# Five moves in the written order of a kernel that joins decaying linear attention to a two-layer feed-forward part: an opening half unit, state decays, key decays and two sums

## The chip, the cores and the metric

The kernel runs on one core of a Trainium2 chip. The metric is device time in microseconds (us); a time of the kernel is the median of several runs. The five engines of the core are named as the profile names them: PE (TensorE, with PEld for its loads of stationary operands), DVE (VectorE), ACT (ScalarE), POOL (GpSimd) and SP (SyncE, which only issues transfers here). Each works through its own queue of instructions in order, and they meet at semaphores.

## The reference

There are two parts, the second fed by the first. The first is attention with a decay in place of a softmax, over q, k, v of shape (4, 8, 768, 64), in blocks of rows with a state that is handed on from block to block:

```
intra = (q_block @ k_block.T * Dmask) @ v_block          # Dmask[i, j] = lam ** (i - j) where i >= j, else 0
inter = (q_block * lam ** (pos + 1)) @ kv_state
out   = intra + inter
kv_state = lam ** block * kv_state + (k_block * lam ** (block - 1 - pos)).T @ v_block
```

The result, laid out as x of shape (3072, 512), goes through a feed-forward part with w_in (512, 2048), w_out (2048, 512) and one slope alpha for each of the 2048 columns:

```
h = x @ w_in
g = maximum(h, 0) + alpha * minimum(h, 0)
out = g @ w_out                                          # float32
```

## The kernel before, in words

**Tiling.** The 3072 rows are cut into 6 chunks of 512 (256 positions of two batches). Attention is cut into 24 units, n = 4c + 2 bi + hh: chunk c, one of its two batches, one half of the heads. Units 4c to 4c+3 together make the input x (`xT`) of chunk c. A unit has two blocks of 128 positions. The feed-forward columns are cut into 16 groups f of 128.

**A unit of attention** is made of these steps, each a small function:

- `load`, `cast` (L307, to 16 bits), `transposes` or `transposed` (q and k turned), `decayed` (L420, the queries with their decay, tile `qdT`) and `key_decayed` (L363, the keys with theirs, tile `kdec`); the last two run mostly on GpSimd.
- `cluster(old, new)`: TensorE's products, in this order: `inter(old)` (L440, queries by state R into the bank `acc`), `score_products(new)` (L458 or L470, into the bank `s`), `intra(old)` (L504, masked scores by values into `acc`) and `state_products(new)` (L524, decayed keys by values into `acc`). There is one bank for `s` and one pair for `acc`.
- `masked` (L485): VectorE multiplies the scores by the decay mask, tile `sm`.
- `attended` (L303): ScalarE copies the result out of `acc` into `xT`.
- `kept` (L553): VectorE adds the new state to the decayed old one, tile R, in up to four instructions; for the first chunks ScalarE copies the first of them (L563). In the opening `state1(n, bank, a)` does the state of one block alone in another bank, started with zeros (L584), so that it needn't wait for `acc`.

**The feed-forward part.** `up(c, f)` makes the products of one column group (L631, four 128x512 products; with a batch given, a half unit of four 128x256 ones), `relu` takes the negative part on ScalarE (L644, tile m) and `act` forms g on VectorE (L655, from m and the product's bank). The products with w_out of the first two chunks are plain (`down`, L668). From chunk 2 on they are done in Strassen's way with seven products of half size in place of eight: `product(c, i, b)` (L825), fed by sums of parts of g (`g_sum`, L808) and of w_out (`weight_sum`, L791). `g_sum(c, i, j, eng)` makes sum i of the column groups 2j and 2j+1 and their partners 2j+8 and 2j+9: i = 1 is called S1 here, i = 2 is S2, which is S1 less another part of g (`g<-s,g` in the profile) and so comes behind S1, i = 3 and 4 are differences of two parts (`g<-g`). The engine is a parameter: "G" for GpSimd, "V" for VectorE. The results go out by `evacuated` (L881, L884) and `written` (L863). In the last chunk the products with w_in are done in the same way (L736).

**The order.** No scheduler orders the work. Some 950 lines of calls, one below the other, are the program (`tc.manual_schedule()`); what a call issues goes to the end of the queue of its engine. To move a call therefore moves its instructions within their own engine's queue, and another engine feels it only through waits. The lines around the five places:

```
    cluster(14, 15)
    attended(14, "A")
    masked(15)
    kept(15)
...
    g_sum(2, 3, 3, "G")
    relu(3, 2, None)
    act(3, 9, None)
    g_sum(2, 2, 3, "G")
    weight_sum(3, 0)
    decayed(18)
```

On-chip accumulators: the banks are named `op`, `tk` and `h` (two buffers) for the feed-forward part and `acc` and `s` for attention; the second product into a bank waits until its last reader is done.

Of the kernel before, what the change touches and what calls it, by code (L numbers as in the profile page):

```python
# [11 lines left out]
def kernel(  # L12
# [72 lines left out]
    def load(c, bi, x, half=None, queue="S"):  # L85

        pb, b = c // 2, 2 * (c % 2) + bi
        if (c, bi) not in raws:
            raws[c, bi] = {}
        if x not in raws[c, bi]:  # L90
            raws[c, bi][x] = (rawv_pool if x == "v" else raw_pool).tile(
                [128, H, 2 * D], fp32, tag=f"{x}raw", name=f"{x}raw"
            )
        heads = ds(0, H) if half is None else ds(4 * half, 4)
        i = "kqv".index(x)
        if x == "k" and c >= HC:
            for a in range(2):
                for f in range(2):
                    nc.sync.dma_start(
                        out=raws[c, bi][x][ds(64 * a, 64), heads, ds(D * f, D)],  # L100
                        in_=k[b, heads, ds(pb * W + L * a + 64 * f, 64), :].rearrange("h p d -> p h d"),
                    )
            return
        (nc.gpsimd if queue == "G" else nc.sync).dma_start(
            out=raws[c, bi][x][:, heads, :],
            in_=(k, q, v)[i][b, heads, ds(pb * W, W), :].rearrange("h (p e) d -> p h (e d)", e=2),
        )
# [193 lines left out]
    def copy_on(eng, out, in_):  # L301
        if eng == "A":
            nc.scalar.activation(out, in_, AF.Copy)  # L303
        elif eng == "V":
            nc.vector.tensor_copy(out=out, in_=in_)
        else:
            nc.gpsimd.tensor_copy(out=out, in_=in_)  # L307
# [8 lines left out]
    def cast(n, name, eng):  # L316
        t = T.setdefault(n, {})
        if name == "v16":
            t[name] = v_of(n)
            c, bi, hh = units[n]  # L320
            copy_on(eng, t[name].rearrange("p h e d -> p h (e d)"), raws[c, bi]["v"][:, ds(4 * hh, 4), :])
            return
        if "qk16" not in t:
            t["qk16"] = half_pool.tile([128, 2, 2, 4, D], fp16, tag="qk16", name="qk16")
        copy_on(eng, t["qk16"][:, int(name == "k16")], raw_of(n)[name])

    V = {}

    def v_of(n):
        c, bi, hh = units[n]  # L330
        if (c, bi) not in V:
            V[c, bi] = v_pool.tile([128, H, 2, D], fp16, tag="v16", name="v16")
        return V[c, bi][:, ds(4 * hh, 4)]
# [24 lines left out]
    def key_decayed(n, eng="G"):  # L358
        hh = units[n][2]
        kr = raw_of(n)["k16"]  # L360
        decay = hdecay if units[n][0] >= HC else kdecay
        kdec = kv_pool.tile([128, 2, 4, D], fp16, tag="kdec", name="kdec")
        engine(eng).tensor_tensor(  # L363
            out=kdec,
            in0=kr,
            in1=decay[:, ds(4 * hh, 4), :].rearrange("p h e -> p e h").unsqueeze(3).to_broadcast([128, 2, 4, D]),
            op=ALU.mult,
        )
        T.setdefault(n, {})["kdec"] = kdec
# [108 lines left out]
    def masked(n):  # L478
        t = T[n]
        t["sm"] = sm_pool.tile([128, 2, 2, 2, L], fp16, tag="sm", name="sm")  # L480
        if units[n][0] >= HC:
            out, in0 = (y.rearrange("p a h x j -> p (a h) (x j)")[:, :, 0:192] for y in (t["sm"], t["s"]))
            nc.vector.tensor_tensor(out=out, in0=in0, in1=HM[units[n][2]], op=ALU.mult)
            return
        nc.vector.tensor_tensor(  # L485
            out=t["sm"].rearrange("p a h x j -> p (a h) x j"),
            in0=t["s"].rearrange("p a h x j -> p (a h) x j"),
            in1=mask_of(units[n][2]),
            op=ALU.mult,
        )  # L490
# [42 lines left out]
    def attended(n, eng):  # L533
        co, bo, ho = units[n]
        if co not in XT:
            XT[co] = xt_pool.tile([128, NHP, 2, 2, L], fp16, tag="xT", name="xT")
        copy_on(
            eng,
            XT[co][:, ds(2 * ho, 2), :, bo, :].rearrange("p h e (a j) -> p a (h e) j", a=2),
            acc[:, :, 0:256].rearrange("p a (he j) -> p a he j", j=64),  # L540
        )
# [24 lines left out]
    def cluster(old, new):  # L566

        if old is not None:
            inter(old)
        if new is not None:  # L570
            score_products(new)
        if old is not None:
            intra(old)
        if new is not None:
            state_products(new, kv_acc, old is None)

    def kept(n):
        states(n, kv_acc)
# [23 lines left out]
    def state1(n, bank, a):  # L602

        t = bank_of(bank, "kv")
        kv = {a: t[:, 0:256].rearrange("p (h l d) -> p h l d", h=2, l=2)}
        beside(kv[a], a)
        state_products(n, kv, False, (a,))
        states(n, kv, (a,))

    G = {}  # L610
# [15 lines left out]
    def up(c, f, bi=None, bank="h"):  # L626
        h_ps = spare[bank] if isinstance(bank, int) else bank_of(bank, "h_ps")
        n = CH if bi is None else W
        for gi in range(NHP):
            x = XT[c][:, gi]  # L630
            nc.tensor.matmul(  # L631
                h_ps[:, 0:n] if bi is None else h_ps[:, 0:n].rearrange("p (e j) -> p e j", e=2),
                lhsT=w_in_sb[:, gi, ts(f, 128)],
                rhs=x.rearrange("p e b j -> p (e b j)") if bi is None else x[:, :, bi, :],
                start=(gi == 0),
                stop=(gi == NHP - 1),
            )
        P[c, f, bi] = h_ps

    def relu(c, f, bi=None):  # L640
        h_ps = P[c, f, bi]
        n = CH if bi is None else W
        m = m_pool.tile([128, CH], fp32, tag="m", name="m")
        nc.scalar.activation(m[:, 0:n], h_ps[:, 0:n], AF.Relu, scale=-1.0)  # L644
        P[c, f, bi] = (m, h_ps)

    def act(c, f, bi=None):
        m, h_ps = P.pop((c, f, bi))
        g = g_of(c, f)
        if bi is None:  # L650
            g, mv, hv = g.rearrange("p e b j -> p (e b j)"), m, h_ps
        else:
            g = g[:, :, bi, :]
            mv, hv = (y[:, 0:W].rearrange("p (e j) -> p e j", e=2) for y in (m, h_ps))
        nc.vector.scalar_tensor_tensor(  # L655
            out=g, in0=mv, scalar=oma[:, f : f + 1], in1=hv, op0=ALU.mult, op1=ALU.add
        )
# [4 lines left out]
    def down(c, t, part, bank):  # L662
        if part == 0:
            O[c, t] = bank_of(bank, "o_ps")
        o_ps = O[c, t]
        n = NF // 4
        for f in range(part * n, part * n + n):
            nc.tensor.matmul(  # L668
                o_ps,
                lhsT=lhs(c, f, t),  # L670
                rhs=w_out_sb[:, f, :],
                start=(f == 0),
                stop=(f == NF - 1),
            )
# [122 lines left out]
    def g_sum(c, i, j, eng, b=None):  # L797

        a11, a12, a21, a22 = [part_of(c, j, half, e, b) for e in range(2) for half in range(2)]
        s1 = sums[3].rearrange("p f (b j) -> p f b j", b=2)[:, ds(2 * j, 2)]  # L800
        s1 = s1.rearrange("p i b j -> p i (b j)") if b is None else s1[:, :, b]
        out, in0, in1, op = {
            1: (s1, a21, a22, ALU.add),
            3: (a21, a11, a21, ALU.subtract),
            2: (a11, s1, a11, ALU.subtract),
            4: (a12, a12, a11, ALU.subtract),
        }[i]
        engine(eng).tensor_tensor(out=out, in0=in0, in1=in1, op=op)  # L808
# [169 lines left out]
    cluster(2, None)  # L978
    attended(2, "A")
    load(1, 1, "q", 1, "G")  # L980
    state1(2, "op", 1)
    state1(3, "tk", 1)
    state1(0, "h", 1)
    cast(4, "q16", "G")
    cluster(3, None)
    attended(3, "A")
    load(1, 1, "k", 1, "G")
    cast(5, "q16", "G")
    up(0, 4, 0, "h")
    relu(0, 4, 0)  # L990
    act(0, 4, 0)
    cast(4, "k16", "G")
    load_v16(5)
# [330 lines left out]
    cluster(13, 14)  # L1324
    attended(13, "A")
    g_sum(2, 3, 0, "G")
    g_sum(2, 3, 1, "G")
    kept(14)
    key_decayed(16, "G")
    down(1, 3, 3, "op")  # L1330
    copied(1, 3)
    masked(14)
# [10 lines left out]
    act(2, 5, None)  # L1343
    cluster(14, 15)
    attended(14, "A")
    masked(15)
    kept(15)
    relu(2, 6, None)
    transposes(16, "D", False)
    cast(19, "k16", "A")  # L1350
# [59 lines left out]
    relu(3, 9, None)  # L1410
    g_sum(2, 3, 3, "G")
    relu(3, 2, None)
    act(3, 9, None)
    g_sum(2, 2, 3, "G")
    weight_sum(3, 0)
    decayed(18)
    act(3, 2, None)
# [92 lines left out]
    act(3, 7, None)  # L1510
    product(2, 4, 0)
    product(2, 4, 1)
    g_sum(3, 3, 2, "V")
    evacuated(2, 4)
    written(2, 4)
    up(3, 15, None, "h")
# [1 line left out]
    relu(3, 15, None)  # L1518
    product(3, 1, 0)
    act(3, 15, None)  # L1520
    g_sum(3, 1, 3, "G")
    up(4, 0, None, "h")
    g_sum(3, 3, 3, "G")
# [351 lines left out]
```

## Time and profile before

| | |
|---|---|
| runs (us) | 205.24, 203.91, 203.53; median 203.91 |
| the profiled execution | 204.43 us, of which the span from the first to the last instruction is 202.6 us |
| granted TensorE clock | 0.999 |
| busy share of the span | PE 97%, PEld 65%, DVE 82%, ACT 57%, POOL 64% |
| chain of work that ended last | PE 86%, DMA 4%, DVE 4%, ACT 2% |
| largest groups of PE | L631 72.8 us, L825 32.9 us with w_out and 15.2 us with its sums, L668 30.3 us |
| transfers | 35.91 MB, 177 GB/s in the mean |

A row of the timeline gives the start (us from the span's start), the busy time, the engine, the line, the operation with its output and inputs, and behind x how many instructions it holds; in brackets stands the idle time just before them and what ended it. A line of the kernel stands for every call of its function, so a place is found by its time and not by its line. The busy time of a group of products on PE overlaps with the next group, since products are pipelined and their ends are modelled; the distance between two starts tells how long a group took.

### The profile page before, as it was taken

The page shows a single profiled execution, that of the slowest core. Times are in us where ns is not written, and L with a number is a line of the kernel's source. Part 1 is how long each engine was busy: PE and PEld are TensorE (multiplying, and loading weights), DVE is VectorE, ACT ScalarE, POOL GpSimd, SP SyncE. Part 2 cuts the span into 40 slices and gives each one's busy share as a digit, 9 for nine tenths or more (in the row PEclk, how much of TensorE's full clock was granted, in tenths as well). Part 3 has the DMA queues.
Part 4 walks back from the last instruction along what each step waited for, and adds up shares of the span by engine and source line. Part 5 has one row for each costly group of instructions (what it writes and reads, how often), then busy time and mean ns, then how long its engine had stood idle before and what let it go on. Part 6 is the DMA issues. An engine that isn't in the chain of part 4 may idle for free.

```text
span 202.6 us, 5876 instructions
## 1 busy us (share of the span) xinstructions
PE 197.4 (97%) x2367; PEld 132.4 (65%) x2367; DVE 165.9 (82%) x311; ACT 116.0 (57%) x228; POOL 130.2 (64%) x155
## 2 busy tenths in 40 slices
PE   7999999999999999999999999999999999999993
PEld 6967445556545456455566666766766788888883
DVE  6888879967788988899999898867797958778931
ACT  7796688336587322765765766544426566665330
POOL 8999895041749879393899968975262239494100
PEclk9999999999999999999999999999999999999999
DMA  5999999997799996899999992999965040101323
GB/s 154 287 193 218 255 272 208 222 291 223 228 222 273 243 238 154 220 207 219 169 170 193 187 274 57 180 245 267 203 128 104 3 155 3 57 0 52 120 77 117
DMA packets 66047, 35.91 MB, mean 177 GB/s; under 512 B 33684, under 2 KB 62500, under 8 KB 66020
## 3 DMA queue, kind: packets, MB, share of 16 engines
q1 hardware_dynamic: 47636, 23.74, 49.5%
q0 software_dynamic: 18080, 11.67, 36.8%
q8 instruction: 18, 0.29, 0.6%
q10 hardware_dynamic: 304, 0.13, 0.2%
q14 instruction: 9, 0.07, 0.1%
HBM read 27.27 MB, written 6.29 MB: 166 GB/s over the span
## 4 chain that ended last, share of the span: by engine, by line
PE 86%; DMA 4%; DVE 4%; ACT 2%; SPq 1%; issue 1%; ACTq 0%
PE h_ps L631 29%; PE o_ps L825 20%; PE o_ps L668 14%; PE up L736 5%; DMA kraw<-in_k_dram 4%; PE unread L167 3%; PE s L470 3%; PE acc L504 2%; PE tpx L406 2%; PE acc L440 2%; DVE g L655 1%; PE up_y L736 1%; PE acc L524 1%; PE up L631 1%; DVE w_out_sb L791 1%; DVE g L808 1%
## 5 line engine op out<-in xcount | busy, mean ns | idle before, releaser
L631 PE MATMUL h_ps<-xT,w_in_sb 128*128 128x512 f16 (+1 forms) x320 | 72.8, 374 | 0.3 <-DVE g L655 0.3
L655 DVE SCALAR_TENSOR_TENSOR g<-m,oma,h_ps 128x512 f16<-128x512 f32 (+1 forms) x80 | 57.6, 730 | 14.3 <-ACT m L644 11.4
L644 ACT ACTIVATE m<-h_ps 128x512 f32<-128x512 f32 (+1 forms) x80 | 46.3, 586 | 32.3 <-PE h_ps L631 30.3
L631 PEld LDWEIGHTS <-w_in_sb 128*128 128x128 f16 x328 | 31.4, 98 | 31.4 <-issue 0.3
L825 PEld LDWEIGHTS <-g 128*128 128x128 f16 x392 | 37.5, 98 | 8.6 <-POOL g L808 0.5
L825 PE MATMUL o_ps<-w_out_sb,g 128*128 128x256 f16 x256 | 32.9, 273 | 0.0
L808 POOL TENSOR_TENSOR g<-g 128x512 f16<-128x512 f16 x20 | 23.3, 1176 | 13.0 <-DVE s L808 12.4
L668 PE MATMUL o_ps<-w_out_sb,g 128*128 128x512 f16 x128 | 30.3, 380 | 0.0
L485 DVE TENSOR_TENSOR sm<-s,dmask 128x1024 f16<-128x1024 f32 x20 | 24.4, 1219 | 5.3 <-PE s L470 5.2
L303 ACT ACTIVATE xT<-acc 128x512 f16<-128x512 f32 x24 | 14.3, 597 | 23.2 <-PE acc L524 19.9
L420 POOL TENSOR_TENSOR qdT<-qkT,qdecay 128x512 f16<-128x512 f16 (+1 forms) x18 | 20.7, 1158 | 3.8 <-DMA qkT<-qk 3.4
L668 PEld LDWEIGHTS <-g 128*128 128x128 f16 x128 | 11.4, 98 | 12.0 <-DVE g L655 0.2
L363 POOL TENSOR_TENSOR kdec<-kraw,kdecay 128x512 f16<-128x512 f32 x14 | 14.6, 1054 | 4.1 <-DMA kraw<-in_k_dram 4.0
L307 POOL CAST qk<-qraw 128x512 f16<-128x512 f32 x12 | 7.8, 651 | 13.5 <-DMA qraw<-in_q_dram 13.4
L553 DVE SCALAR_TENSOR_TENSOR R<-R,rdecay,acc 128x128 f16<-128x128 f16 x54 | 15.5, 339 | 0.1
L825 PE MATMUL o_ps<-w_sum,g 128*128 128x256 f16 x120 | 15.2, 273 | 0.2 <-POOL g L808 0.2
L881 ACT ACTIVATE o_sb<-o_ps 128x512 f32<-128x512 f32 (+1 forms) x20 | 10.2, 509 | 8.7 <-PE o_ps L825 6.9
L808 POOL TENSOR_TENSOR s<-g 128x512 f16<-128x512 f16 x7 | 8.1, 1158 | 7.3 <-DVE g L655 7.3
L884 DVE TENSOR_TENSOR o_sb<-o_sb,o_ps 128x512 f32<-128x512 f32 (+1 forms) x15 | 8.5, 574 | 4.7 <-PE o_ps L825 2.2
L644 ACT ACTIVATE m<-up 128x512 f32<-128x512 f32 x14 | 8.3, 597 | 7.1 <-PE up L736 5.4
L349 POOL DMA_DIRECT2D v<-in_v_dram x15 | 11.9, 803 | 0.1
L307 POOL CAST qk<-kraw 128x512 f16<-128x512 f32 x9 | 6.5, 722 | 8.1 <-DMA kraw<-in_k_dram 8.1
(127 smaller groups left out, 299.5 us busy)
## 6 DMA issues: line engine op xcount, KB each, us to landing
out_dram<-o_sb SPq DMA_DIRECT2D x20, 256.0 KB, 2.7
qraw<-in_q_dram SPq DMA_DIRECT2D x6, 512.0 KB, 5.6
kraw<-in_k_dram SPq DMA_DIRECT2D x5, 512.0 KB, 7.2
w_in_sb<-in_moe_w_in_dram POOLq DMA_DIRECT2D x4, 512.0 KB, 7.7
w_out_sb<-in_moe_w_out_dram POOLq DMA_DIRECT2D x4, 512.0 KB, 10.3
wi_sum<-w_in_sb SPq DMA_DIRECT2D x4, 512.0 KB, 3.9
v<-in_v_dram POOLq DMA_DIRECT2D x15, 128.0 KB, 5.3
qraw<-in_q_dram POOLq DMA_DIRECT2D x6, 256.0 KB, 6.7
```

Source lines behind the costliest of these rows:

```text
L303: nc.scalar.activation(out, in_, AF.Copy)
L307: nc.gpsimd.tensor_copy(out=out, in_=in_)
L363: engine(eng).tensor_tensor(out=kdec, in0=kr, in1=decay[:, ds(4 * hh, 4), :].rearrange("p h e -> p e h").unsqueeze(3).to_broadcast([128, 2 ...
L420: engine(eng).tensor_tensor(out=qdT[:, :, :, p], in0=(t["qps"] if eng == "P" else t["qkT"][:, 0])[:, :, :, p], in1=qdecay[:, hh, :, :, p], ...
L485: nc.vector.tensor_tensor(out=t["sm"].rearrange("p a h x j -> p (a h) x j"), in0=t["s"].rearrange("p a h x j -> p (a h) x j"), in1=mask_of ...
L553: nc.vector.scalar_tensor_tensor(out=R[b, hh, m + 1][:, hp], in0=R[b, hh, m][:, hp], scalar=rdecay[:, 2 * hh + hp : 2 * hh + hp + 1], in1= ...
L631: nc.tensor.matmul(h_ps[:, 0:n] if bi is None else h_ps[:, 0:n].rearrange("p (e j) -> p e j", e=2), lhsT=w_in_sb[:, gi, ts(f, 128)], rhs=x ...
L644: nc.scalar.activation(m[:, 0:n], h_ps[:, 0:n], AF.Relu, scale=-1.0)
L655: nc.vector.scalar_tensor_tensor(out=g, in0=mv, scalar=oma[:, f : f + 1], in1=hv, op0=ALU.mult, op1=ALU.add)
L668: nc.tensor.matmul(o_ps, lhsT=lhs(c, f, t), rhs=w_out_sb[:, f, :], start=(f == 0), stop=(f == NF - 1),)
L808: engine(eng).tensor_tensor(out=out, in0=in0, in1=in1, op=op)
L825: nc.tensor.matmul(t, lhsT=x, rhs=w, start=(fresh and f == 0), stop=(last and f == NF // 2 - 1), skip_group_check=True,)
```

## The change

Five places in the written order change; no function changes, no work is added or taken away, and the order on SP is the same.

```diff
     load(1, 1, "q", 1, "G")
+    cast(4, "q16", "G")
+    up(0, 4, 0, "h")
+    relu(0, 4, 0)
     state1(2, "op", 1)
+    cluster(3, None)
+    attended(3, "A")
     state1(3, "tk", 1)
     state1(0, "h", 1)
-    cast(4, "q16", "G")
-    cluster(3, None)
-    attended(3, "A")
     load(1, 1, "k", 1, "G")
     cast(5, "q16", "G")
-    up(0, 4, 0, "h")
-    relu(0, 4, 0)
     act(0, 4, 0)
...
     g_sum(2, 3, 0, "G")
-    g_sum(2, 3, 1, "G")
     kept(14)
     key_decayed(16, "G")
+    g_sum(2, 3, 1, "G")
     down(1, 3, 3, "op")
...
     attended(14, "A")
+    kept(15)
     masked(15)
-    kept(15)
     relu(2, 6, None)
...
     relu(3, 2, None)
+    g_sum(2, 2, 3, "V")
     act(3, 9, None)
-    g_sum(2, 2, 3, "G")
     weight_sum(3, 0)
...
     product(2, 4, 1)
-    g_sum(3, 3, 2, "V")
     evacuated(2, 4)
...
     act(3, 15, None)
+    g_sum(3, 3, 2, "V")
     g_sum(3, 1, 3, "G")
```

The prediction numbers the five moves: 1 is the opening; 2 the decays of unit 15 (`kept(15)`) ahead of its mask; 3 the keys of unit 16 ahead of a g sum; 4 the S2 sum `g_sum(2, 2, 3)` from GpSimd to VectorE; 5 the sum `g_sum(3, 3, 2)` behind two ReLU products.

**Opening, ScalarE (move 1).** In the opening of the program, ScalarE's queue around the copies of units 2 and 3 (`xT<-acc`), the half unit's negative part (`m<-h_ps 128x256`) and the first whole one's (`m<-h_ps 128x512`):

```order
 L303 ACTIVATE xT<-acc 128x2x4x64
 L563 ACTIVATE R_1_1_114<-kv 128x256
-L303 ACTIVATE xT<-acc 128x2x4x64 x2
+L303 ACTIVATE xT<-acc 128x2x4x64
 L644 ACTIVATE m<-h_ps 128x256
+L303 ACTIVATE xT<-acc 128x2x4x64
 L644 ACTIVATE m<-h_ps 128x512
 L644 ACTIVATE m<-h_ps 128x256
```

The half unit now stands between the copies of units 2 and 3. On PE its four products stand behind the `intra` of unit 2 and ahead of one of the three one-block states; the products of unit 3's attention stand behind that state, with the other two states behind them.

**Unit 15, VectorE (move 2).** VectorE's queue at the mask of unit 15 (`sm<-s,dmask`) and its four decays (`R<-R,rdecay,acc`), with what each instruction waits for. Before:

```order
L655 SCALAR_TENSOR_TENSOR g_2065<-m,oma,h_ps 128x512 [waits Activation_49] x3
L485 TENSOR_TENSOR sm<-s,dmask 128x1024 [waits PE_49]
L553 SCALAR_TENSOR_TENSOR R_1_1_126<-R_1_2_127,rdecay,acc 128x128 [waits Activation_49]
L553 SCALAR_TENSOR_TENSOR R_1_1_126<-R_1_2_127,rdecay,acc 128x128
L553 SCALAR_TENSOR_TENSOR R_1_4_128<-R_1_1_126,rdecay,acc 128x128 [waits DVE_49] x2
L655 SCALAR_TENSOR_TENSOR g_2156<-m,oma,h_ps 128x512 [waits Activation_49]
```

And of the change:

```order
L655 SCALAR_TENSOR_TENSOR g_2065<-m,oma,h_ps 128x512 [waits Activation_49] x3
L553 SCALAR_TENSOR_TENSOR R_1_1_126<-R_1_2_127,rdecay,acc 128x128 [waits Activation_49]
L553 SCALAR_TENSOR_TENSOR R_1_1_126<-R_1_2_127,rdecay,acc 128x128
L553 SCALAR_TENSOR_TENSOR R_1_4_128<-R_1_1_126,rdecay,acc 128x128 [waits DVE_49] x2
L485 TENSOR_TENSOR sm<-s,dmask 128x1024
L655 SCALAR_TENSOR_TENSOR g_2156<-m,oma,h_ps 128x512 [waits Activation_49]
```

The four decays come first, with the wait for ScalarE that they had before, and the mask, which waited for PE alone, now stands behind them and that wait.

**The S2 sum (move 4).** The piece of VectorE's queue around the S2 sum of column groups 6 and 7 of chunk 2 (`g_2156<-s_1948,g_2156`):

```order
 L553 SCALAR_TENSOR_TENSOR R_1_1_108<-R_1_4_110,rdecay,acc 128x128 x2
 L808 TENSOR_TENSOR g_2065<-s_1948,g_2065 128x2x256
+L808 TENSOR_TENSOR g_2156<-s_1948,g_2156 128x2x256
 L655 SCALAR_TENSOR_TENSOR g_2267<-m,oma,h_ps 128x512
 L791 TENSOR_TENSOR w_out_sb<-w_out_sb 128x4x256
```

It leaves GpSimd's queue, where it stood ahead of the query decay of unit 18 (`decayed(18)`), and goes ahead of a ReLU product and of the first weight sum on VectorE.

## The prediction, made before the changed kernel was run

> **What bounds the kernel now.** I read the page's busy times first, then the chain that ended last, then TensorE's own timeline, because only the moments in which TensorE stands still can be won or lost.
>
> ```profile
> PE 197.4 (97%) x2367; PEld 132.4 (65%) x2367; DVE 165.9 (82%) x311; ACT 116.0 (57%) x228; POOL 130.2 (64%) x155
> PE 86%; DMA 4%; DVE 4%; ACT 2%; SPq 1%; issue 1%; ACTq 0%
> ```
>
> TensorE is busy for 97% of the span and carries 86% of the chain. The change adds no work to it, so the question is where it waits near the edited places. TensorE's timeline there (start, duration, operation, count, idle time before):
>
> ```profile
> 17.36 0.29 PE L440 MATMUL acc<-qdT,R 128*128 128x128 f16 x2 [0.16 <-ACT xT L303]
> 97.29 2.76 PE L631 MATMUL h_ps<-xT,w_in_sb 128*128 128x512 f16 x12
> 100.17 0.38 PE L440 MATMUL acc<-qdT,R 128*128 128x128 f16 x4
> 100.48 0.42 PE L470 MATMUL s<-qkT 64*64 64x128 f16 x16
> 101.14 0.31 PE L524 MATMUL acc<-v,kdec 64*64 64x64 f16 x8
> 101.39 0.81 PE L631 MATMUL h_ps<-xT,w_in_sb 128*128 128x512 f16 x3
> 110.33 1.02 PE L631 MATMUL h_ps<-xT,w_in_sb 128*128 128x512 f16 x4
> 111.19 0.82 PE L825 MATMUL o_ps<-w_sum,g 128*128 128x256 f16 x6
> 112.19 1.05 PE L825 MATMUL o_ps<-w_sum,g 128*128 128x256 f16 x8 [0.19 <-POOL g L808]
> 120.93 0.81 PE L631 MATMUL h_ps<-xT,w_in_sb 128*128 128x512 f16 x3 [0.33 <-DVE g L655]
> ```
>
> The starts say more than the idle times, since ends are modelled. Four 128x512 products take 111.19 - 110.33 = 0.86, so one takes 0.216 and a 128x256 one 0.108. Twelve from 97.29 end at 99.88, but the next starts at 100.17: 0.28 lost. Six from 111.19 end at 111.84, the next starts at 112.19: 0.35 lost, waiting for a sum on GpSimd. At 120.93 about 0.4 is lost to a VectorE product. These waits and the one at 17.36 come to some 1.4 us: this is all that edits of order can win here.
>
> **Edit 1, the half unit in the opening.**
>
> ```profile
> 16.24 0.42 PE L504 MATMUL acc<-sm,v 64*64 64x128 f16 x16
> 16.49 0.22 PE L584 MATMUL kv<-zeros 64*64 64x128 f16 x2
> 17.58 0.42 PE L504 MATMUL acc<-sm,v 64*64 64x128 f16 x16
> 17.93 1.26 PE L631 MATMUL h_ps<-xT,w_in_sb 128*128 128x256 f16 x7
> 16.71 0.60 ACT L303 ACTIVATE xT<-acc 128x512 f16<-128x512 f32 x1 [0.28 <-PE acc L504]
> 18.05 0.60 ACT L303 ACTIVATE xT<-acc 128x512 f16<-128x512 f32 x1 [0.74 <-PE acc L504]
> 17.29 1.63 DVE L553 SCALAR_TENSOR_TENSOR R<-R,rdecay,kv 128x128 f16<-128x128 f16 x6
> 20.07 1.14 DVE L655 SCALAR_TENSOR_TENSOR g<-m,oma,h_ps 128x512 f16<-128x512 f32 x2 [0.60 <-ACT m L644]
> ```
>
> From L504 to the next 64-row work takes 16.49 - 16.24 = 0.25, to 128-row work 17.93 - 17.58 = 0.35: a turn costs 0.10. Three state products fill 16.49 to about 17.04, so 0.18 each. Now the half unit comes first: 16.24 + 0.35 = 16.59, four products to 17.03, a turn, one state to 17.31, a turn, unit 3's first product at 17.41. ScalarE's copy of unit 2, which it waits for, ends at 17.31, so the wait is gone, yet the start is 0.05 later than 17.36: the two extra turns took its place. From there 0.22 and 0.25 to the two remaining states, 0.36 for them and a turn bring the whole unit 6 to 18.34, where it stood at 17.93 + 0.44 = 18.37. Gain: 0.03. Its third product needs ScalarE's copy of unit 3, which moves with TensorE to 18.70 and is in time for 18.34 + 0.43 = 18.77. The decays on VectorE follow the states and push the half unit's product 0.3 later; the 0.60 idle before 20.07 hides that. The queues keep their order. Bounds: -0.15 (no turn paid behind the states) to +0.15 (that copy late as well). I take -0.03.
>
> **Edits 2 and 3, decays ahead of the mask and keys ahead of a g sum.** VectorE, ScalarE, then GpSimd:
>
> ```profile
> 97.11 0.75 DVE L655 SCALAR_TENSOR_TENSOR g<-m,oma,h_ps 128x512 f16<-128x512 f32 x1 [0.32 <-ACT m L644]
> 97.77 1.22 DVE L485 TENSOR_TENSOR sm<-s,dmask 128x1024 f16<-128x1024 f32 x1
> 98.91 1.11 DVE L553 SCALAR_TENSOR_TENSOR R<-R,rdecay,acc 128x128 f16<-128x128 f16 x4
> 99.94 2.06 DVE L655 SCALAR_TENSOR_TENSOR g<-m,oma,h_ps 128x512 f16<-128x512 f32 x3
> 97.42 0.60 ACT L303 ACTIVATE xT<-acc 128x512 f16<-128x512 f32 x1 [0.34 <-PE acc L524]
> 97.80 2.27 POOL L808 TENSOR_TENSOR g<-g 128x512 f16<-128x512 f16 x2
> 100.03 2.06 POOL L363 TENSOR_TENSOR kdec<-kraw,kdecay 128x512 f16<-128x512 f32 x2
> ```
>
> TensorE's start at 100.17 follows the last decay's end at 100.02. With the decays first it can go at 99.88. But the program makes unit 15's decays wait for ScalarE's copy of unit 14, 97.42 to 98.02; the mask had no such wait. VectorE reaches them at 97.77 and stands until 98.05. That is 0.28 of new idle time, and all behind it moves: the mask to 99.08 and its end to 100.30, the three products to 100.22. The score products of unit 16 wait for the mask, so they start at 100.35 instead of 100.48: 0.13 won. The keys' decay on GpSimd now ends near 99.97 instead of 101.08, so the state products at 101.14 lose their wait of 0.18. Then comes the loss. The up product at 101.39 starts 0.05 behind the second of VectorE's three products (99.94 + 0.66 + 0.74 = 101.34), whose bank it takes. That product now ends at 101.62, so TensorE starts at 101.67: +0.28, with both gains spent in front of it. The g sum that the keys overtake is read at 108.07 at the earliest, 6 us later: 0. Bounds: -0.3 (if the copy came early enough) to +0.3.
>
> **Edit 4, one S2 sum to VectorE.** Before pricing it, see how such sums run beside GpSimd:
>
> ```profile
> 105.54 1.29 DVE L808 TENSOR_TENSOR s<-g 128x512 f16<-128x512 f16 x1
> 110.72 0.41 DVE L808 TENSOR_TENSOR g<-s,g 128x512 f16<-128x512 f16 x1
> 112.08 0.75 DVE L655 SCALAR_TENSOR_TENSOR g<-m,oma,h_ps 128x512 f16<-128x512 f32 x1 [0.95 <-ACT m L644]
> 112.74 1.07 DVE L791 TENSOR_TENSOR w_out_sb<-w_out_sb 128x1024 f16<-128x1024 f16 x1
> 114.99 0.69 DVE L791 TENSOR_TENSOR w_out_sb<-w_out_sb 128x1024 f16<-128x1024 f16 x1
> 118.82 1.39 DVE L808 TENSOR_TENSOR g<-g 128x512 f16<-128x512 f16 x1
> 104.22 2.31 POOL L420 TENSOR_TENSOR qdT<-qkT,qdecay 128x512 f16<-128x512 f16 x2
> 110.69 1.44 POOL L808 TENSOR_TENSOR g<-s,g 128x512 f16<-128x512 f16 x1
> 112.10 1.16 POOL L420 TENSOR_TENSOR qdT<-qkT,qdecay 128x512 f16<-128x512 f16 x1
> 115.15 1.56 POOL L420 TENSOR_TENSOR qdT<-qkT,qdecay 128x512 f16<-128x512 f16 x1
> 118.79 1.15 POOL L808 TENSOR_TENSOR s<-g 128x512 f16<-128x512 f16 x1
> ```
>
> A sum of 0.41 takes 1.29 or 1.39 when GpSimd is in an operation, and ends 0.28 behind that operation's end (106.53, 119.94); a weight sum of 0.69 ends 0.55 behind (113.26 to 113.81). The other way round GpSimd takes 1.44 or 1.56. They exclude each other. The Trainium skill says so (SBUF — State Buffer, Who interferes with whom): whichever issues first holds the shared port pair for the whole instruction. At 110.69 GpSimd is first by 0.03 and yet the one stretched, so for near ties the row decides; by that rule the sum below would be the same.
>
> The lock first helps: VectorE, 0.28 late, meets the query decay that ends at 106.53 all the same, and is on time again at 106.82. TensorE, without a pause from 101.39 to 110.3, keeps its 0.28 and starts the unit at 110.33 at 110.60. Now GpSimd, rid of its sum (1.44), starts the next query decay at 110.57 and holds the port to 111.73: VectorE's sum of 110.72 ends at 112.01, the moved one at 112.35, and TensorE's product that needs it goes at 112.40 instead of 112.19. So the wait of 0.35 shrinks to 0.28 and TensorE is 0.2 late. VectorE's idle 0.95 covers the moved sum: its next product would start at 112.31 anyway, behind TensorE and ScalarE.
>
> Behind it two weight sums meet GpSimd's shifted work. The first is locked out by the key decay (now 112.5 to 113.6) and ends at 114.1 instead of 113.8. The second, at 115.3, meets the query decay that a transpose landing near 115.0 releases. If GpSimd is first, that sum ends at 116.8, not 115.7, and the unit of TensorE that follows VectorE there starts 0.6 late, of which the old pause of 0.4 ahead of 120.93 takes up 0.4; the sum at 118.82 is again absorbed by the lock. The unit at 120.93 then starts near 121.1: +0.2. If VectorE is first, the old wait of 0.4 swallows TensorE's 0.2, and the start lies between 120.7 and 121.0: -0.2 to +0.05. The starts are within 0.3 us of each other, so I weigh both alike and take +0.1 at this point. Bounds for edits 2 to 4 together: -0.2 to +0.9, the upper one if nothing absorbs VectorE's delay.
>
> **Edit 5, one sum behind two ReLU products.**
>
> ```profile
> 134.01 0.75 DVE L655 SCALAR_TENSOR_TENSOR g<-m,oma,h_ps 128x512 f16<-128x512 f32 x1 [0.87 <-ACT m L644]
> 135.75 0.75 DVE L655 SCALAR_TENSOR_TENSOR g<-m,oma,h_ps 128x512 f16<-128x512 f32 x1 [0.99 <-ACT m L644]
> ```
>
> The sum moves from 132.06 into the idle 0.99 ahead of 135.75, where 0.41 fits. TensorE shows no wait around here, so nothing is won: 0. If GpSimd's next sum took the port first, the product at 135.75 would slip by 0.4 and TensorE by up to 0.3: the bound.
>
> **Sum.** -0.03 + 0.1 + 0 is about +0.1 us. The profiled execution took 204.43 us, 1.8 of them outside its span of 202.6; it lies 0.5 above the median of the timed runs, 203.91. So: span 202.7, a median of **204.0 us**.
>
> **The rivals.** *All waits pay* (faster): the copy does not hold the decays, VectorE is never late, and 0.28 + 0.18 + 0.35 + 0.40 go, 1.2 us: 202.7. For it: each of these waits is on TensorE. Against it: 101.39 and 120.93 hang on VectorE, which gets more to do, not less. *The port cascade* (slower): GpSimd wins the port at 115.1, the delay of 0.87 at VectorE's product of 117.0 is not absorbed at 118.8, TensorE stands until 121.8, and the sum of edit 5 loses the port too (0.3): 1.2 us, 205.1. It decides from the point where the query decay at 115.1 starts before the weight sum. For it: 1.07 and 1.39 in the rows above; against it: a lock also absorbs, as at 105.54. *Nothing moves*: the edits lie in idle time, 203.9; the order of the program shows that they are made, so only their worth can vanish.
>
> **How the numbers follow.** Forecast with *nothing moves*, 203.6 to 204.4: 0.67. All waits pay, whole or half: 0.13. Cascade, whole or half: 0.20. The range 202.7 to 205.1 reaches to both other cases whole, since the runs of one kernel alone lie 1.7 us apart, and holds the forecast's bounds. About 1% (2.0 us) is what a measurement can tell from no change here. No case reaches it. On the faster side the waits on TensorE, 1.4 us in all, are a limit, so only the spread of runs could carry the time there: 0.05. On the slower side there is no such limit, as a late VectorE product can hold TensorE again and again: 0.13, a part of the cascade's 0.20. Same: 0.82.
>
> **What would show it.** Edit 1: L440 still near 17.4, the whole unit within 0.1 of 18.37. Edit 2: about 0.3 idle on VectorE before the decays, released by ScalarE, and TensorE at 101.7. Edit 3: no wait before the state products. Edit 4: the S2 sum at 110.7 takes about 1.3, and TensorE's wait at 112.2 stays in part. Behind 121 every TensorE start is shifted alike. Wrong if TensorE's shift grows behind 121, if the decays start at 97.8 without a wait, or if the total moves by more than 1.2 us.

## The result, and the profile after

The changed kernel takes 205.5 us in the median of 19 runs (204.96 to 208.21), the kernel before 204.35 us in 19 runs (203.53 to 206.1; the three runs behind the prediction had a median of 203.91). The ratio is 1.0053, with a 95% interval of 1.0034 to 1.0072: 1.1 us slower, about half a percent. (The run of 208.21 is a slow one, with a granted clock of 0.992, and is left out of the ratio.) Forecast were 204.0 us, a gain or loss within 1%, and a range that ended at 205.1, 0.4 too low.

The page of the profiled execution (205.06 us, span 203.3 us), its busy times and its chain of work:

```profile
PE 196.7 (97%) x2367; PEld 131.8 (65%) x2367; DVE 166.9 (82%) x312; ACT 115.9 (57%) x228; POOL 128.3 (63%) x154
PE 85%; DVE 5%; POOL 4%; DMA 4%; issue 0%; ACT 0%; POOLq 0%
```

One instruction went from POOL to DVE, the S2 sum. TensorE is no busier. So the time is again in its pauses, and one of them stands out in its timeline (a few rows of it):

```profile
109.82 0.71 PE L825 MATMUL o_ps<-w_out_sb,g 128*128 128x256 f16 x5
110.36 1.03 PE L631 MATMUL h_ps<-xT,w_in_sb 128*128 128x512 f16 x4
111.23 0.82 PE L825 MATMUL o_ps<-w_sum,g 128*128 128x256 f16 x6
113.21 1.26 PE L825 MATMUL o_ps<-w_sum,g 128*128 128x256 f16 x10 [1.17 <-DVE g L808]
121.32 0.29 PE L524 MATMUL acc<-v,kdec 64*64 64x64 f16 x8
121.55 0.82 PE L631 MATMUL h_ps<-xT,w_in_sb 128*128 128x512 f16 x3
```

The product that reads the moved S2 sum starts at 113.21. Before, it started at 112.19, when the sum was still GpSimd's. The six products ahead of it, from 111.23, would be done near 111.88 at the 0.108 each of the prediction, so TensorE stood for some 1.3. The pause of 0.4 ahead of the unit at 120.93 is gone (121.32 to 121.55 has no bracket), and that unit starts 0.62 later than before. From there the shift stays (0.63 at the products of 139.01, before 138.38).

What VectorE, then GpSimd did around the S2 sums, from the timeline:

```profile
109.98 3.18 DVE L808 TENSOR_TENSOR g<-s,g 128x512 f16<-128x512 f16 x2
113.08 0.73 DVE L655 SCALAR_TENSOR_TENSOR g<-m,oma,h_ps 128x512 f16<-128x512 f32 x1
109.85 1.16 POOL L420 TENSOR_TENSOR qdT<-qkT,qdecay 128x512 f16<-128x512 f16 x1
110.96 0.83 POOL L349 DMA_DIRECT2D v<-in_v_dram  x1
111.80 1.06 POOL L363 TENSOR_TENSOR kdec<-kraw,hdecay 128x512 f16<-128x512 f32 x1
```

The same two sums in the view of their tile (shortest, middle and longest duration in ns):

```profile
L808 DVE TENSOR_TENSOR g<-s,g x2: 1315/1627/1939, 110.0 to 111.2; 128x512 f16<-128x512 f16 x2
```

Two sums that take 0.41 each with nothing in their way took 3.18 us. I say that a VectorE sum is held when it lasts until behind the end of a GpSimd operation. The first met the query decay of unit 18 (`decayed(18)`, 109.85 to 111.01) and ended 0.28 behind it, at 111.29. The second has its start recorded at 111.22, while GpSimd was issuing a transfer (`load_v16(19)`). It ended at 113.16, 0.29 behind the end of the next GpSimd work, the key decay of unit 20 (`key_decayed(20)`, 111.80 to 112.86).

### The profile page after: what moved, and what is told of

It reads as the page before. It is cut to its first block, busy times and chain, and to the rows that moved or that the text cites. A ratio compares the mean times of both kernels' runs of the same rounds, so it can differ in the third digit from the quotient of the medians.

```text
span 203.3 us, 5878 instructions
## 1 busy us (share of the span) xinstructions
PE 196.7 (97%) x2367; PEld 131.8 (65%) x2367; DVE 166.9 (82%) x312; ACT 115.9 (57%) x228; POOL 128.3 (63%) x154
## 4 chain that ended last, share of the span: by engine, by line
PE 85%; DVE 5%; POOL 4%; DMA 4%; issue 0%; ACT 0%; POOLq 0%
PE h_ps L631 31%; PE o_ps L825 23%; PE o_ps L668 14%; PE up L736 5%; DMA w_in_sb<-in_moe_w_in_dram 4%; PE s L470 3%; PE acc L504 2%; PE acc L440 2%; DVE g L808 2%; POOL v L349 1%; DVE sm L485 1%; PE up_y L736 1%; PE acc L524 1%; DVE g L655 1%; PE tpx L406 1%; PE up L631 1%
## 5 line engine op out<-in xcount | busy, mean ns | idle before, releaser
L655 DVE SCALAR_TENSOR_TENSOR g<-m,oma,up 128x512 f16<-128x512 f32 x14 | 10.2, 744 | 1.5 <-ACT m L644 1.5
```

The source lines that it names most:

```text
L655: nc.vector.scalar_tensor_tensor(out=g, in0=mv, scalar=oma[:, f : f + 1], in1=hv, op0=ALU.mult, op1=ALU.add)
```

## The experiments

The theory: that key decay holds the second sum, and this is the loss. The rivals: the loss lies in edits 1 to 3, or it is spread over all. Each profile below is one execution of its kernel; the times are medians of 12 runs. Each kernel below is compared with runs of the kernel before on the same chip.

**The edits one by one.**

```diff
 e1_opening:      the first hunk of the change alone (half unit, cluster(3), attended(3))
 e2_decays_keys:
-    g_sum(2, 3, 1, "G")
     kept(14)
     key_decayed(16, "G")
+    g_sum(2, 3, 1, "G")
...
+    kept(15)
     masked(15)
-    kept(15)
 e4_s2sum:
+    g_sum(2, 2, 3, "V")
     act(3, 9, None)
-    g_sum(2, 2, 3, "G")
 e5_sum:
-    g_sum(3, 3, 2, "V")
     evacuated(2, 4)
...
     act(3, 15, None)
+    g_sum(3, 3, 2, "V")
```

> Only edit 1 (the half unit sooner). Theory: the half unit's first product now waits for the first transfer of w_in, which lands at 16.3 to 16.4 whatever TensorE does; where TensorE reaches it early (15.95 in the profile of the change) 0.4 us is lost, where it comes late nothing: +0.2 to +0.4 us in the median. Rival, the prediction's own working: -0.03, no difference. Second rival: the two extra turns of TensorE alone, at most +0.1.

> Only edits 2 and 3 (decays ahead of the mask, keys ahead of a g sum). Theory: TensorE's unit at 101.4 starts 0.28 later behind VectorE, and the old waits at 112.2 and 120.9 take it up: within 0.1 us of before. Rival: they bring GpSimd forward so that the S2 sums meet its query decay, with GpSimd's own S2 sum still in its queue: up to +0.5 us at 112.2.

> Only edit 4 (the S2 sum on VectorE). Theory: two S2 sums back to back on VectorE are locked out in a row, first by a query decay, then by the next key decay, which is let in during the transfer that GpSimd issues between them; TensorE's product at 112.2 starts 0.6 to 1.0 us later, 0.4 of it taken up ahead of 120.9: +0.4 to +0.6 us. Rival, the prediction's working: one lock alone, +0.2 at 112.2, 0 to +0.2 at the end. Second rival: VectorE alone does it without a lock, -0.3.

> Only edit 5 (one sum behind two ReLU products). Both theories: nothing, within 0.1 us of before. Rival: GpSimd's next sum takes the port first and TensorE loses up to 0.3 us near 136.

| kernel | median us | ratio to before | 95% interval |
|---|---|---|---|
| edit 1 | 204.91 | 1.0021 | 0.9996 to 1.0046 |
| edits 2 and 3 | 205.02 | 1.0023 | 0.9998 to 1.0048 |
| edit 4 | 205.33 | 1.0035 | 1.0016 to 1.0054 |
| edit 5 | 204.75 | 1.0012 | 0.9988 to 1.0037 |

Only edit 4 is slower clear of noise; its +0.7 us (0.3 to 1.1) is somewhat above the 0.4 to 0.6 expected of the double hold, which lies in that interval. Edit 1 alone comes out at +0.4, as expected, and edits 2 and 3 alone at +0.5, where the theory had expected 0.1 at most and its rival up to 0.5; both intervals hold no difference too. In the profile of edit 4 alone the two sums take 1309 and 1945 ns (view of the tile):

```profile
L808 DVE TENSOR_TENSOR g<-s,g x2: 1309/1627/1945, 110.4 to 111.6; 128x512 f16<-128x512 f16 x2
```

and TensorE's product starts at 113.61 (timeline):

```profile
113.61 0.61 PE L825 MATMUL o_ps<-w_sum,g 128*128 128x256 f16 x4 [1.48 <-DVE g L808]
```

The profile of edit 5 was the surprise. Up to 132 us its program is that of the kernel before, and yet it shows a pause that the profile before did not have. VectorE, GpSimd and TensorE there:

```profile
112.98 2.17 DVE L791 TENSOR_TENSOR w_out_sb<-w_out_sb 128x1024 f16<-128x1024 f16 x1
112.68 0.83 POOL L349 DMA_DIRECT2D v<-in_v_dram  x1
113.53 1.06 POOL L363 TENSOR_TENSOR kdec<-kraw,hdecay 128x512 f16<-128x512 f32 x1
115.86 1.02 PE L631 MATMUL h_ps<-xT,w_in_sb 128*128 128x512 f16 x4 [0.75 <-DVE g L655]
```

Here it is the weight sum, 0.69 when nothing is in its way, that begins while the same transfer is issued, and it takes 2.17, to 0.56 behind the key decay's end. The profiles of edit 1 alone and of edits 2 and 3 alone show it too (2.17 each). In the profile before, the weight sum had begun at 112.74, ahead of the query decay's end (113.26), and got in between that decay and the key decay.

**The change without edit 4.**

```diff
-    g_sum(2, 2, 3, "V")
     act(3, 9, None)
+    g_sum(2, 2, 3, "G")
```

> The whole change without edit 4. Theory (the S2 sum carries most of the loss): within 0.3 us of before, some 0.7 below the change. Rival (the loss is spread over the edits, and the S2 sum only takes the lock that the weight sum would meet otherwise): as slow as the change, +0.8 to +1.1.

204.95 us, ratio 1.0032 (1.0008 to 1.0057). Neither reading holds whole: the time lies between the two, and against the change (1.0053) it is not clear of noise. In its profile the weight sum takes 2.17 us: without the moved sum, the key decay holds the next VectorE sum.

**What holds it: the transfer or the key decay.** Both kernels are the whole change, with one GpSimd step moved.

```diff
 x1_change_v_behind:
-    load_v16(19)
     product(2, 6, 0)
     key_decayed(20)
+    load_v16(19)
 x2_change_keys_behind:
     product(2, 6, 0)
-    key_decayed(20)
...
     decayed(19)
+    key_decayed(20)
```

> The change, with GpSimd's transfer of unit 19's values moved behind the key decay of unit 20, so that no transfer stands between the query decay of unit 18 and that key decay. Theory (a sum that begins while this transfer is issued is held to the end of the key decay): the second S2 sum still meets the key decay, which is now 0.8 earlier, and ends 0.8 earlier, at 112.3 against 113.16; TensorE's product behind it likewise; some -0.4 us against the change, since 0.4 was taken up ahead of 120.9. Rival (the sum waits for something else than the port): nothing.

> The change, with the key decay of unit 20 moved behind the query decay of unit 19, so that the transfer is followed by no GpSimd work for 3 us. Theory A (it is the key decay that holds the port): the second S2 sum takes 0.4, TensorE's product starts near 111.9. Theory B (the issue of the transfer itself holds the port): the sum ends 0.3 to 0.6 behind the issue, near 112.1 to 112.4. Rival (neither): 1.9 us as before. Time: -0.4 to -0.7 us against the change by A or B, nothing by the rival, unless the later key decay delays the sums behind it by 1.1.

With the transfer behind (x1): 205.11 us, ratio 1.0021 (0.9995 to 1.0047). The two sums, in the view of their tile:

```profile
L808 DVE TENSOR_TENSOR g<-s,g x2: 1264/1287/1310, 110.7 to 111.9; 128x512 f16<-128x512 f16 x2
```

VectorE, GpSimd, and TensorE's product in the timeline:

```profile
110.68 2.50 DVE L808 TENSOR_TENSOR g<-s,g 128x512 f16<-128x512 f16 x2
111.67 1.23 POOL L363 TENSOR_TENSOR kdec<-kraw,hdecay 128x512 f16<-128x512 f32 x1
112.85 0.83 POOL L349 DMA_DIRECT2D v<-in_v_dram  x1
113.24 1.26 PE L825 MATMUL o_ps<-w_sum,g 128*128 128x256 f16 x10 [0.80 <-DVE g L808]
```

The pair takes 2.50 in place of 3.18, 0.7 less where 0.8 was expected, and again it ends 0.28 behind the key decay. But in this execution the pair began 0.70 later, so TensorE's product stands where it stood, and the expected 112.3 was missed: the pair ends at 113.18. What it gained against the change is not clear of noise.

With the key decay behind (x2): 204.24 us, ratio to before 0.9991 (0.9965 to 1.0018). The sums, in the view of their tile:

```profile
L808 DVE TENSOR_TENSOR g<-s,g x2: 412/868/1323, 109.9 to 111.2; 128x512 f16<-128x512 f16 x2
```

GpSimd and TensorE in the timeline:

```profile
109.83 1.16 POOL L420 TENSOR_TENSOR qdT<-qkT,qdecay 128x512 f16<-128x512 f16 x1
110.93 0.83 POOL L349 DMA_DIRECT2D v<-in_v_dram  x1
115.83 1.16 POOL L420 TENSOR_TENSOR qdT<-qkT,qdecay 128x512 f16<-128x512 f16 x1 [4.07 <-DMA qkT<-qk]
111.19 1.91 PE L825 MATMUL o_ps<-w_sum,g 128*128 128x256 f16 x16
```

The timing is that of the change, to 0.04 us: query decay at 109.83, transfer at 110.93, second sum during its issue. Only the key decay is missing behind it, and the sum takes 412 ns. TensorE runs its sixteen products without a pause. So it is the key decay that holds the sum, and not the transfer alone. Against the change this is 0.9991 / 1.0053 = 0.9938, interval about 0.991 to 0.997 (both half widths, added as squares), or 1.3 us: all of the loss. Some of it the kernel before may pay too, since the same move there (y2, below) gives 0.9987, not clear of no difference.

**The same move in kernels with fewer of the edits.** The key decay stands behind as in x2, but for y1, which is the kernel before with the transfer behind as in x1.

```diff
 y1_before_v_behind       = before, load_v16(19) behind key_decayed(20)
 y2_before_keys_behind    = before, key_decayed(20) behind decayed(19)
 z3_s2_alone_keys_behind  = y2 + edit 4
 z2_s2_keys_behind        = z3 + edit 3
 z1_no_opening_keys_behind = z2 + edits 2 and 5
 w1_no_s2_keys_behind     = y2 + edits 1, 2, 3 and 5
```

> The kernel before, with that same transfer behind the key decay. Theory: where its weight sum at 113.0 begins during the issue and takes 2.17 (three of the profiles with GpSimd's S2 sum in place), it now takes 1.3 to 1.4: -0.3 to -0.5 us in the median against before. Rival: the wait is taken up elsewhere, no difference.

> The kernel before, with the key decay of unit 20 behind the query decay of unit 19 as in x2_change_keys_behind. Theory (in the kernel before too that key decay holds a VectorE sum, the weight sum at 113, in most executions): the weight sum takes 0.7 to 1.1, TensorE loses nothing at 115 to 116; -0.3 to -0.6 us in the median. Rival (what TensorE loses there comes back at 112.2 and 120.9 in any case): within 0.2 us of before.

> Edit 4 alone, with that key decay behind. Theory (edit 4 is harmful only by the key decay's lock): the second S2 sum takes 0.41; the old wait of 0.35 at 112.2 shrinks to nothing or 0.1: 0 to -0.4 us against y2_before_keys_behind, and 0.6 to 1.0 us below edit 4 alone (e4_s2sum). Rival: VectorE's added work delays its products, +0.2 or more against y2_before_keys_behind.

> Edits 3 and 4, with that key decay behind. Theory: the wait of 0.18 ahead of the state products at 101.1 is gone or taken up behind; 0 to -0.2 us against z3_s2_alone_keys_behind. Rival: no difference, since the start of the next unit at 101.4 is set by VectorE.

> Edits 2 to 5, with that key decay behind. Theory: the decays' new wait for ScalarE makes the unit at 101.4 start 0.28 later, part of it taken up behind: 0 to +0.3 us against z2_s2_keys_behind; and without edit 1 the half unit no longer waits for the first transfer of w_in: 0 to -0.3 us against x2_change_keys_behind. Rival: both differences below 0.1.

> Edits 1, 2, 3 and 5 (the S2 sum stays on GpSimd), with the key decay of unit 20 behind the query decay of unit 19. Theory (what the change without edit 4 lost, 0.32%, is the weight sum held by the same key decay): the weight sum takes 0.7 to 1.1, no wait of TensorE near 115.9, and the time is within 0.1% of the kernel before, 0.2 to 0.3% below e6_all_but_s2. Rival (edits 1 to 3 lose it themselves, at the opening and at 101.5): +0.2 to +0.3% as in e6_all_but_s2, though the weight sum is short.

| kernel | median us | ratio to before | 95% interval |
|---|---|---|---|
| y1 | 204.7 | 1.0011 | 0.9987 to 1.0035 |
| y2 | 203.99 | 0.9987 | 0.9961 to 1.0012 |
| z3 | 204.12 | 0.9988 | 0.9970 to 1.0006 |
| z2 | 204.32 | 1.0003 | 0.9980 to 1.0026 |
| z1 | 203.75 | 0.9977 | 0.9957 to 0.9996 |
| w1 | 204.75 | 1.0020 | 0.9995 to 1.0045 |

y1 missed: its weight sum took 1.07 in an execution in which it had begun early, and the later transfer made TensorE wait for it:

```profile
121.16 0.31 PE L524 MATMUL acc<-v,kdec 64*64 64x64 f16 x8 [0.80 <-DMA v<-in_v_dram]
```

Edit 4 alone goes from 1.0035 to 0.9988 once the key decay is out of the way (z3): a ratio of 0.9953, interval about 0.993 to 0.998, or 1.0 us, the upper end of what was expected. What is left between the kernels of this table, w1 apart, is within the noise of each step. Several steps came out on the other side of what was expected, by no more than that noise: z3 is 0.1 above y2 (expected 0 to 0.4 below), z2 0.2 above z3 (0 to 0.2 below), z1 0.6 below z2 (0 to 0.3 above). y2 itself, at -0.3 us, lies at the edge of its theory (-0.3 to -0.6) and near its rival (within 0.2). The gain that the prediction's first rival promised, 1.2 us, is not there: z1 is below before by 0.23%, with an interval that just excludes no difference, one of six in the table. Against z1, the change has edit 1 in addition and the key decay in its old place. w1 did not settle its question: its weight sum is short (0.68) and TensorE has no wait near 115.9, but 1.0020 lies between the theory and the rival.

**The hold in all profiles.** The median times carry the whole kernel's noise; the profiles show the place itself. In all seven with the moved sum, the first of the pair took 1.30 to 1.32. The second took 1.26 to 1.95 in the three with the key decay next (the change, edit 4 alone, x1) and 0.41 in the four with it behind (x2, z1, z2, z3). The time from TensorE's unit at 110 to its unit at 121, start to start, holds the same work in all fifteen:

| kernels | unit at 110 to unit at 121, us |
|---|---|
| S2 sum on GpSimd, key decay in its old place (before; edits 2 and 3; edit 5; the change without edit 4; edit 1) | 10.60; 10.89; 10.83; 10.76; 11.59 |
| S2 sum moved, key decay in its old place (the change; edit 4; x1) | 11.19; 11.99; 11.19 |
| key decay behind (x2; w1; z1; y2; z3; z2) | 9.84; 9.85; 10.11; 10.19; 10.26; 10.71 |
| y1, transfer moved | 11.19 |

Where the key decay stands behind, the moved sum costs this stage little (9.84 to 10.71 with it, 9.85 and 10.19 without); where it stands in its old place, 11.19 to 11.99 with the moved sum stand against 10.60 to 10.89 in four of five without (edit 1 alone has a second pause, of 0.79 at 117.98).

## Where the prediction was right and where it failed

**The step that failed** is in edit 4: "the moved one at 112.35", with TensorE at 112.40. I charged the pair of sums one hold, by the query decay, and let the second follow the first at once. By my own numbers GpSimd would then be issuing a transfer, between the query decay's end at 111.73 and the key decay at 112.5; I took that gap as free for the second sum, and gave no reason. It was held again, by the key decay that stands behind that transfer, and TensorE started at 113.21, 0.8 later than forecast. The pause ahead of 120.93 took up its 0.4 as I had reckoned, and the rest went to the end. I had priced a cascade of locks (1.2 us), but I let it decide at the weight sum of 115, and gave it 0.20. There it did not come:

```profile
115.59 0.68 DVE L791 TENSOR_TENSOR w_out_sb<-w_out_sb 128x1024 f16<-128x1024 f16 x1
115.87 1.43 POOL L420 TENSOR_TENSOR qdT<-qkT,qdecay 128x512 f16<-128x512 f16 x1 [3.01 <-DMA qkT<-qk]
```

VectorE was first by 0.28, and the weight sum took its 0.68. The sum that decided is the one that stands ahead of unit 20's key decay: the moved S2 sum here, the weight sum at 113 where S2 stays on GpSimd. That the measured time is near the cascade's 205.1 bears out neither its place nor its chance.

**The first hold went as forecast**, 1.31 against 0.41, but in part by luck, since the route was another. I had let VectorE meet the query decays at 105.5 and lose its 0.28 in that lock. It met none, and TensorE's unit at 110 started at 110.36, not at 110.60. GpSimd in the timeline of before:

```profile
96.80 1.05 POOL L363 TENSOR_TENSOR kdec<-kraw,kdecay 128x512 f16<-128x512 f32 x1 [2.93 <-DMA kraw<-in_k_dram]
```

and GpSimd, then VectorE, in that of the change:

```profile
94.93 1.05 POOL L363 TENSOR_TENSOR kdec<-kraw,kdecay 128x512 f16<-128x512 f32 x1 [1.21 <-DMA kraw<-in_k_dram]
102.35 2.31 POOL L420 TENSOR_TENSOR qdT<-qkT,qdecay 128x512 f16<-128x512 f16 x2
105.67 0.42 DVE L808 TENSOR_TENSOR s<-g 128x512 f16<-128x512 f16 x1
```

The keys' transfer, on which GpSimd waits in both, let it go 1.87 sooner in this execution, so GpSimd's query decays ran 1.87 ahead of where they had been (102.35 for 104.22), and VectorE's S1 sum took 0.42 in place of 1.29. No edit stands near that transfer. In six profiles whose program is that of before up to this place (before, edit 4, edit 5, y1, y2, z3), that wait ended at six times from 95.29 to 96.80. The S1 sum took 1.09 to 1.30 in the five of the fifteen profiles whose query decays began at 103.88 or later, and 0.41 to 0.63 in the ten others. Which sums meet which decays at this place differs from execution to execution with that landing, and I had read one draw as the kernel's own schedule.

**Edits 2 and 3 were right to a tenth.** TensorE, then VectorE:

```profile
97.15 2.76 PE L631 MATMUL h_ps<-xT,w_in_sb 128*128 128x512 f16 x12
99.75 0.39 PE L440 MATMUL acc<-qdT,R 128*128 128x128 f16 x4
100.31 0.42 PE L470 MATMUL s<-qkT 64*64 64x128 f16 x16 [0.17 <-DVE sm L485]
100.76 0.32 PE L524 MATMUL acc<-v,kdec 64*64 64x64 f16 x8
101.53 0.81 PE L631 MATMUL h_ps<-xT,w_in_sb 128*128 128x512 f16 x3 [0.46 <-DVE g L655]
97.91 1.12 DVE L553 SCALAR_TENSOR_TENSOR R<-R,rdecay,acc 128x128 f16<-128x128 f16 x4 [0.20 <-ACT xT L303]
```

The decays wait for ScalarE's copy, the two small waits of TensorE (ahead of L440 and of L524) are gone, and the unit behind starts 101.53 - 97.15 = 4.38 after the one at 97, where it was 4.10: +0.28, the number forecast. Their gains were spent in front of a product that VectorE sets. The score products came 0.03 sooner and not 0.13, which changed nothing behind them. All seven profiles with edit 2 show 4.38 to 4.40 here, and the eight without it 4.09 to 4.10.

**Edit 1 was not -0.03.** The half unit's products in the change (timeline):

```profile
16.35 0.61 PE L631 MATMUL h_ps<-xT,w_in_sb 128*128 128x256 f16 x4 [0.33 <-DMA w_in_sb<-in_moe_w_in_dram]
```

and in edit 1 alone:

```profile
16.38 0.61 PE L631 MATMUL h_ps<-xT,w_in_sb 128*128 128x256 f16 x4 [0.37 <-DMA w_in_sb<-in_moe_w_in_dram]
```

I had put the start at 16.59 and never asked when the weights land: by these rows at 16.3 to 16.4, a margin of 0.2 against 16.59, and none in an execution whose opening runs 0.6 sooner. In all six profiles with edit 1 these products, or the load of their weights (0.22 in x2), wait for that transfer, and they start at 16.35 to 16.48. The first score products behind the opening stand at 32.28 to 32.41 in those six (mean 32.33), and at 31.95 to 32.53 in the nine without it (mean 32.19). The edit gives up the early starts: some +0.14 by the profiles, which the runs can't tell from nothing.

**Edit 5** cost TensorE nothing, as forecast: 0 within its interval, and the sum sits in idle time of the change:

```profile
135.31 0.42 DVE L808 TENSOR_TENSOR g<-g 128x512 f16<-128x512 f16 x1
136.38 1.61 DVE L655 SCALAR_TENSOR_TENSOR g<-m,oma,h_ps 128x512 f16<-128x512 f32 x2 [0.65 <-ACT m L644]
```

**The baseline**: the three runs shown had a median 0.44 below that of 19. The absolute miss of 1.5 is made of this 0.44, of about 0.5 at the S2 sum (TensorE's unit at 121 came 0.62 late, where +0.1 was forecast), and of about 0.5 that no profile here places: the profiled execution of the change, 205.06, is itself 0.44 below the median of its runs.

**What stays open.** How much of the kernel before's own time is that hold: its profile shows none, four profiles of kernels with the S2 sum and the key decay where it has them do (edits 1, 2 and 3, 5, and all but 4), and y2 is below it by 0.13% with an interval on both sides. And why the change without edit 4 is slower by 0.3%: its weight sum is held as in the three others, while w1 did not come all the way back. The 0.28 of edit 2 and the 0.14 of edit 1 add to 0.4 us, which is what w1 lost; but x2 holds these edits too and lost nothing, so this is a guess. Nor is it shown by what means a key decay holds a sum that is on record ahead of it.

## What to carry to other kernels

Two engines that lock each other out are one queue: before a step moves from one to the other, lay out both queues side by side and ask of every operation near it what stands next on the other engine; a transfer that is issued in between was no gap here. A pause that one profile shows on the busiest engine may be a draw of that execution; where it hangs on when a transfer lands, take a second profile, or shift that landing by some tenths and look again before pricing it. And a step that is moved ahead needs its operands' landing checked, not only the engine's place for it.

## What the runs showed of the hardware

- A VectorE sum whose recorded start lies 0.5 to 0.6 ahead of the recorded start of a GpSimd decay was held until behind that decay's end, in all six profiles in which it began during the transfer's issue at 111 to 113 with the key decay next in GpSimd's queue (1.94 and 1.95 for a sum of 0.41, 2.17 four times for a sum of 0.69). With no decay next, they took 0.41 (x2) and 0.68 (y2). The Trainium skill (SBUF — State Buffer, Who interferes with whom) lets the one that issues first have the shared port pair; by the recorded starts VectorE was first, so the measurement decides: it is as if a GpSimd operation that is next in line had the port before its record begins. A recorded start need not be the moment of issue, so whether the rule or the record is off is not shown. The same section of the Trainium skill infers that a two-input sum does not contend with the writing of descriptors for a transfer, and x2 agrees with 412 ns. It does not happen behind every transfer: in the profile before, a sum at 129.44 began during the issue of a smaller one, with a key decay next at 129.81, and took 0.46. What differs there was not tried.
- The opening does not run alike in each execution. The same 45 warm-up products, in the timeline of before:

```profile
5.22 3.77 PE L167 MATMUL unread<-ident 128*128 128x128 f16 x45
```

  and of the change:

```profile
5.22 3.13 PE L167 MATMUL unread<-ident 128*128 128x128 f16 x45
```

  They begin alike and last 0.64 longer in one execution; the steps from start to start fall from 107 to 56 ns at 7.5 in the profile before, and at 6.2 in that of the change. In the fifteen profiles the next products start anywhere from 7.74 to 8.83. The Trainium skill (TensorE: Matmul & The Clock Gate, Part 1) says that TensorE's clock opens by a free-running window, so that the point varies from run to run; the two rows agree. The profile on which the prediction rests was the latest of the fifteen, and this hid the wait of edit 1.
